# A cached-attention decode block on one core: the first softmax in pieces among K's last half tiles, three transfers fewer, and f32 matmuls without a reader

## The chip, the cores and the metric

The kernel runs on one core of a Trainium2 chip. The metric is the device time in microseconds of one execution. The core's engines work side by side, each through its own list of instructions in order: TensorE (PE; the loading of weights into it is shown as PEld), VectorE (DVE), ScalarE (ACT), GpSimd (POOL) and SyncE (SP), which here issues every transfer. The engines wait for each other and for transfers through semaphores. The profile also gives the granted TensorE clock: 1.0 is full speed, and the records of this kernel show 1.0 and 0.5.

## The reference, cut to what matters

One decode step for two batch elements, with 32 heads of 192, a window of the last 1024 keys, and a feed-forward layer after it; all inputs are bf16.

```python
mod = (silu(c) @ w_mod).reshape(2, 6, 1, 640)          # sa, ca, ga, sb, cb, gb
h = layernorm(x) * (1 + ca) + sa
q = (h @ wq).reshape(2, 1, 32, 192).transpose(0, 2, 1, 3)
k, v = k_cache[:, :, -1024:, :], v_cache[:, :, -1024:, :]
p = softmax(einsum('bhqd,bhkd->bhqk', q, k) * 192 ** -0.5)
o = einsum('bhqk,bhkd->bhqd', p, v)
x = x + ga * (o.transpose(0, 2, 1, 3).reshape(2, 1, 6144) @ wo)
h = layernorm(x) * (1 + cb) + sb
x = x + gb * ((gelu(h @ w_gate) * (h @ w_up)) @ w_down)
```

K and V of the window are 25.2 MB each, and with the weights 76.9 MB are read from HBM.

## The kernel before, in words

**Order.** A small planner (`_Sched`) collects operations; each engine's list is the order in which the code calls them. It works out from the buffers that an operation reads and writes what it must wait for. A PSUM bank counts as written by everyone who touches it. Nothing is reordered, so an operation that waits holds up everything behind it on its engine.

**Transfers.** All are issued by SP, in the order of the code, and go through one queue: w_mod, c and x, wq (7680 KB), then K of batch 0 in two loads of two tiles (6144 KB each), K of batch 1 in two, V of batch 0 in two, V of batch 1 in one load of two tiles and two loads of one tile (L336, L337), wo in four pieces of 16, 16, 12 and 4 of its 48 row tiles, w_gate, w_up, and w_down in three. A load waits on SP until the buffer that it fills has been read: the V loads wait for reduces of K, the last V loads for the first PV of batch 0, wo for the last PV of batch 0, the feed-forward weights for the first two PV of batch 1.

**Scores.** A cache tile has 128 partitions (32 heads by 4 groups of keys) with 64 keys of 192 each. Each tile is worked in two halves. For a half (b, t, hf), `d_mul` (L465, VectorE) multiplies K by the broadcast q in place, `p_reduce` (L476) adds up in TensorE with an identity as weights (12 matmuls of 512 columns), and `d_rows` (L483, VectorE) adds the rest from PSUM into `S_sb`. `scores` calls `d_rows` one half late, so VectorE multiplies the next half while TensorE reduces this one. Ahead of each reduce stands `filler()`: four bf16 matmuls of 384 columns whose result nobody reads (`warm`, L454).

**Softmax.** `softmax(b)` (L487) is a chain through three engines: pmax (DVE), a transpose on TensorE, max and gx (DVE), a broadcast matmul Bc, nb (DVE), exp (ACT), a matmul den, and its reciprocal rden (DVE). Both softmaxes run one after the other once all scores are done (L577, L578).

**PV and after.** `d_mask` (L511, VectorE) spreads a tile's probabilities over the heads into one of two buffers `Em`, `p_pv` (L523) multiplies by V with 32 matmuls. After batch 0's four tiles `normalize(0)` scales the result; after batch 1's, `normalize(1)`. `p_sel` puts both batches together, `oc` moves the result out of PSUM, three transposes `oT` (L597) on VectorE prepare 16 row tiles of wo each, and the wo matmuls (L628) follow by pieces. Then come the second layer norm (`layer_norm("ln2", 1, 3)`), the w_gate matmuls, gelu, the w_up matmuls, geglu (L660), its transpose, the w_down matmuls by pieces (L669), and the output. Between these stand further `warm` calls.

Of the kernel before, what the change touches and what calls it, by code (L numbers as in the profile page):

```python
# [5 lines left out]
ALU = mybir.AluOpType  # L6
ACTF = mybir.ActivationFunctionType
AX = mybir.AxisListType
# [95 lines left out]
def bass_adaLN_cond__sliding_block_cached__geglu_ffn__decode_kernel(  # L104
# [15 lines left out]
    P = 128  # L120
    B, _, D = A_x.shape
    _, H, Sk, Dh = A_k_cache.shape
# [9 lines left out]
    DN = D // NJ  # L132
# [3 lines left out]
    QP = P // H  # L136
# [10 lines left out]
    SCALE = float(Dh) ** -0.5  # L147
# [6 lines left out]
    NS = 4  # L154
    SL = J * Dh
    WQ_SPLIT = [5]
    assert sum(WQ_SPLIT) == KT
    WO_SPLIT = [16, 16, 12, 4]
    OT_SPLIT = [16, 16, 16]
    assert sum(WO_SPLIT) == NT and sum(OT_SPLIT) == NT  # L160
    WU_SPLIT = [5]
    assert sum(WU_SPLIT) == KT
    WD_SPLIT = [6, 4, 2]
    assert sum(WD_SPLIT) == FT
    ND = 4

    WO_WARM = [0, 8, 0, 9]
    WU_WARM = [5]
    WD_WARM = [5, 0, 0]

    es = ExitStack()
    with es:
        S = _Sched(nc, es)
# [45 lines left out]
        DS = sb("DS", [P, P], F32)  # L219
# [8 lines left out]
        modC = sb("modC", [P, 6, DN], F32)  # L228
# [10 lines left out]
        M1 = sb("M1", [P, 1], F32)  # L239
# [19 lines left out]
        def bank(k):  # L259
            return ("bank", k)  # L260
# [9 lines left out]
        sem_ring = [S.sem("d_ring%d" % i) for i in range(4)]  # L270
        sem_out = S.sem("d_out")

        def k_dma(dst, src):
# [49 lines left out]
        def ring_keys(slot):  # L323
# [10 lines left out]


        items = [("k", 0, 0, 2, 0, 0), ("k", 0, 2, 2, 2, 1), ("k", 1, 0, 2, NS, 2), ("k", 1, 2, 2, 0, 0), ("v", 0, 0, 2, 2, 1),  # L336
                 ("v", 0, 2, 2, NS, 2), ("v", 1, 0, 2, 0, 0), ("v", 1, 2, 1, 2, 1), ("v", 1, 3, 1, 3, 3)]  # L337
        place = {(kind, b, t0 + i): slot + i for kind, b, t0, nt, slot, _ in items for i in range(nt)}
        assert NTL == 4 and len(place) == 4 * NTL

# [109 lines left out]
        def warm(n, bk):  # L450
            def f(e):
                last = None
                for _ in range(n):
                    last = e.matmul(ps[:, bk, 0:2 * Dh], lhsT=ident_b[:, :], rhs=qbc[:, :, :].rearrange("p b d -> p (b d)"),  # L454
                                    start=True, stop=True)
                return last
            if n:
                S.op("pe", f, reads=["ident_b", "qbc"], writes=[bank(bk)], name="warm")
# [22 lines left out]
        def d_rows(b, t, hf):  # L481
            a = J * t + JH * hf
            S.op("dve", lambda e: e.tensor_reduce(out=S_sb[:, b, a:a + JH], in_=ps[:, hf, 0:JH * GC].rearrange("p (j c) -> p j c", j=JH),  # L483
                                                  axis=AX.X, op=ALU.add),
                 reads=[bank(hf)], writes=[("S", b, t, hf)], name="rows%d_%d_%d" % (b, t, hf))

        def softmax(b):  # L487
            sk = [("S", b, t, hf) for t in range(NTL) for hf in range(2)]
            S.op("dve", lambda e: e.tensor_reduce(out=M1[:, :], in_=S_sb[:, b, :], axis=AX.X, op=ALU.max),
                 reads=sk, writes=["M1"], name="pmax%d" % b)  # L490
            S.op("pe", lambda e: e.transpose(ps[0:1, BK_T, 0:P], M1[:, :], ident_f[:, :]),  # L491
                 reads=["M1", "ident_f"], writes=[bank(BK_T)], name="T%d" % b)
            S.op("dve", lambda e: e.tensor_reduce(out=gm[:, :], in_=ps[0:1, BK_T, 0:P].rearrange("k (h t) -> k h t", t=QP), axis=AX.X, op=ALU.max),
                 reads=[bank(BK_T)], writes=["gm"], name="max%d" % b)
            S.op("dve", lambda e: e.tensor_scalar(out=gx[:, :, :], in0=gm[:, :].unsqueeze(2).broadcast_to([1, H, QP]),
                                                  scalar1=-SCALE, scalar2=None, op0=ALU.mult),
                 reads=["gm"], writes=["gx"], name="gx%d" % b)
            S.op("pe", lambda e: e.matmul(ps[:, BK_T, P:P + 1], lhsT=gx[:, :, :].rearrange("k h t -> k (h t)"), rhs=one[:, :],  # L498
                                          start=True, stop=True),
                 reads=["gx", "one"], writes=[bank(BK_T)], name="Bc%d" % b)  # L500
            S.op("dve", lambda e: e.tensor_copy(out=nb[:, :], in_=ps[:, BK_T, P:P + 1]), reads=[bank(BK_T)], writes=["nb"], name="nb%d" % b)  # L501
            S.op("act", lambda e: e.activation(out=E_sb[:, b, :], in_=S_sb[:, b, :], func=ACTF.Exp, scale=SCALE, bias=nb[:, 0:1], accum_out=esum[:, b:b + 1]),  # L502
                 reads=sk + ["nb"], writes=[("E", b), ("esum", b)], name="exp%d" % b)
            S.op("pe", lambda e: e.matmul(ps[:, BK_T, P + 2:P + 3], lhsT=DS[:, :], rhs=esum[:, b:b + 1], start=True, stop=True),  # L504
                 reads=[("esum", b), "DS"], writes=[bank(BK_T)], name="den%d" % b)
            S.op("dve", lambda e: e.reciprocal(out=rden[:, b:b + 1], in_=ps[:, BK_T, P + 2:P + 3]),
                 reads=[bank(BK_T)], writes=[("rden", b)], name="rden%d" % b)


        def d_mask(b, t):  # L510
            S.op("dve", lambda e: e.tensor_tensor(out=Em[:, t % 2, :, :], in0=E_sb[:, b, J * t:J * (t + 1)].unsqueeze(2).broadcast_to([P, J, H]),  # L511
                                                  in1=M32b[:, :].unsqueeze(1).broadcast_to([P, J, H]), op=ALU.mult),
                 reads=[("E", b), "M32b"], writes=[("Em", t % 2)], name="mask%d_%d" % (b, t))

        def p_pv(b, t):
            vs = slot_of("v", b, t)
            n = J // 2

            def f(e):
                last = None  # L520
                for jp in range(n):
                    r = 2 * SQ * (jp % 2)
                    last = e.matmul(ps[r:r + 2 * H, BK_O, 0:ON],  # L523
                                    lhsT=Em[:, t % 2, 2 * jp:2 * jp + 2, :].rearrange("p j c -> p (j c)"),
                                    rhs=tile_v(vs)[:, 2 * jp:2 * jp + 2, :],
                                    start=(t == 0 and jp < 2), stop=(t == NTL - 1 and jp >= n - 2), tile_position=(0, r), skip_group_check=True)
                return last
            keep[("pv", b, t)] = S.op("pe", f, reads=[("Em", t % 2)] + ring_keys(vs), writes=[bank(BK_O)], name="PV%d_%d" % (b, t))
# [64 lines left out]
        for c in range(NQC):  # L593
            move(("act", "dve")[c % 2], oc[:, QC * c:QC * (c + 1)], ps[:, BK_H + c, 0:QC], [bank(BK_H + c)], [("oc", c)], "oc%d" % c)
# [121 lines left out]
```

## Time and profile before

| what | value |
|---|---|
| median of 3 runs | 187.17 us (187.05 to 187.21) |
| the profiled execution's own time | 187.01 us |
| its span, first to last instruction | 185.7 us |
| mean granted TensorE clock | 0.915 |
| PE busy | 117.2 us (63%) |
| DVE busy | 106.6 us (57%) |
| ACT busy | 13.9 us (7%) |
| moved by the DMA engines | 77.02 MB, mean 415 GB/s |

Busy times of different engines overlap, so they do not add up to the span. A line of the timeline gives start and length in us, the engine, the line of the code, the operation with what it writes and reads, how many instructions were merged (x12), and in brackets how long the engine was idle before and who released it. A row with x2 f32 under PE is one f32 matmul in the code: it appears as two records. Times in the text without another mark are counted from the start of the span.

### The profile page before, as it was taken

To read this page: it belongs to the slowest core of one execution; us is meant where nothing else is said; L and a number is where in the kernel's file an instruction comes from. 1 tells how busy PE (TensorE), PEld (TensorE's weight loads), DVE (VectorE), ACT (ScalarE), POOL (GpSimd) and SP (SyncE) were. 2 spreads that over 40 slices of the span, in tenths; PEclk is the share of its full clock that TensorE was granted. 3 is DMA by queue.
4 is the path that set the end of the run, shared out by engine and by line. 5 is a ranking of instruction groups with operands and counts; after the bars stand their busy time and mean duration, and the time that the engine had idled before them with its cause. 6 is when DMAs were issued, how large, how long until landed. Compare 5 with 4: busy or idle time off the path is not lost.

```text
span 185.7 us, 2254 instructions
## 1 busy us (share of the span) xinstructions
PE 117.2 (63%) x1014; PEld 60.8 (33%) x1014; DVE 106.6 (57%) x114; ACT 13.9 (7%) x24; POOL 4.9 (3%) x12
## 2 busy tenths in 40 slices
PE   0004500871079899988999885349928977299844
PEld 0001200440024334433344342226614654265422
DVE  6801600020598999999999993294556714803331
ACT  2001400013000000000000000200010004100400
POOL 8200000000000000000000000000000000000000
PEclk9999999998559999999999999558996999859999
DMA  7999998898999989899999989899999999999991
GB/s 248 414 437 477 463 463 389 371 491 371 487 413 434 468 381 459 381 487 402 455 424 434 459 381 466 381 487 413 395 434 424 424 435 424 413 408 435 422 392 50
DMA packets 2925, 77.02 MB, mean 415 GB/s; under 512 B 356, under 2 KB 356, under 8 KB 868
## 3 DMA queue, kind: packets, MB, share of 16 engines
q1 hardware_dynamic: 2916, 76.88, 96.7%
q8 instruction: 8, 0.13, 0.3%
q14 instruction: 1, 0.01, 0.0%
HBM read 76.88 MB, written 0.00 MB: 414 GB/s over the span
## 4 chain that ended last, share of the span: by engine, by line
DMA 43%; DVE 36%; PE 16%; SPq 1%; ACT 1%; issue 1%; POOL 1%; DVEq 0%; POOLq 0%
DMA ring<-in_A_k_cache_dram 24%; DVE ring L465 19%; DMA ring<-in_B_w_down_dram 18%; PE ps L523 10%; DVE r L465 7%; DVE Sg L483 5%; PE ps L476 4%; DVE Em L511 2%; SPq L274 1%; ACT E_sb L502 1%; PE ps L504 1%; PE ps L498 1%; DVE On L540 0%; ACT On L536 0%; PE ps L491 0%
## 5 line engine op out<-in xcount | busy, mean ns | idle before, releaser
L465 DVE TENSOR_TENSOR ring<-ring,qbc 128x6144 bf16<-128x6144 bf16 x12 | 40.1, 3351 | 8.4 <-DMA ring<-in_A_k_cache_dram 8.4
L476 PE MATMUL ps<-ring,ident_b 128*128 128x512 bf16 x144 | 34.7, 393 | 13.0 <-DVE ring L465 13.0
L454 PE MATMUL ps<-qbc,ident_b 128*128 128x384 bf16 x120 | 24.7, 339 | 0.7 <-ACT qbc L432 0.7
L523 PE MATMUL ps<-ring,Em 128*64 128x384 bf16 x192 | 19.6, 371 | 7.8 <-DVE Em L511 6.6
L476 PEld LDWEIGHTS ps<-ring,ident_b 128*128 128x128 bf16 x144 | 13.6, 100 | 32.7 <-DVE ring L465 17.2
L511 DVE TENSOR_TENSOR Em<-E_sb,M32b 128x2048 bf16<-128x2048 bf16 x8 | 18.1, 2288 | 5.5 <-PE ps L523 5.5
L523 PEld LDWEIGHTS ps<-ring,Em 128*64 128x64 bf16 x192 | 12.4, 125 | 14.6 <-DVE Em L511 7.3
L454 PEld LDWEIGHTS ps<-qbc,ident_b 128*128 128x128 bf16 x120 | 11.6, 101 | 10.9 <-issue 2.8
L401 PE MATMUL ps<-ring,scT 128*32 128x480 bf16 x40 | 4.4, 601 | 16.0 <-DVE scT L358 16.0
L465 DVE TENSOR_TENSOR r<-r,qbc 128x6144 bf16<-128x6144 bf16 x4 | 13.4, 3352 | 0.0
L483 DVE TENSOR_REDUCE Sg<-ps 128x32 f32<-128x512 f32 x16 | 11.0, 687 | 3.4 <-PE ps L476 3.4
L424 PE MATMUL ps<-r,hT 128*32 128x384 bf16 x80 | 5.8, 475 | 10.7 <-DMA r<-in_A_wq_dram 10.7
L476 PE MATMUL ps<-r,ident_b 128*128 128x512 bf16 x48 | 11.1, 380 | 1.8 <-DVE r L465 1.8
L434 DVE CAST aux<-ps 128x384 bf16<-128x384 f32 x4 | 2.0, 553 | 16.6 <-PE ps L424 15.7
L628 PE MATMUL ps<-r,aux 128*32 128x160 bf16 x192 | 5.1, 271 | 4.4 <-DMA r<-in_A_wo_dram 2.6
L424 PEld LDWEIGHTS ps<-r,hT 128*32 128x32 bf16 x80 | 3.2, 135 | 13.8 <-issue 11.6
L476 PEld LDWEIGHTS ps<-r,ident_b 128*128 128x128 bf16 x48 | 4.4, 98 | 8.1 <-DVE r L465 3.4
L401 PEld LDWEIGHTS ps<-ring,scT 128*32 128x32 bf16 x40 | 1.2, 132 | 17.5 <-DVE scT L358 16.0
L540 DVE TENSOR_SCALAR On<-ps,rden 32x192 bf16<-32x192 f32 x4 | 1.7, 418 | 8.9 <-ACT On L536 8.9
L502 ACT ACTIVATE E_sb<-Sg,nb 128x256 bf16<-128x256 f32 x2 | 1.0, 507 | 75.6 <-DVE nb L501 75.6
L628 PEld LDWEIGHTS ps<-r,aux 128*32 128x32 bf16 x192 | 4.3, 114 | 5.8 <-DMA r<-in_A_wo_dram 3.6
L523 PE MATMUL ps<-r,Em 128*64 128x384 bf16 x64 | 5.4, 327 | 0.0
(73 smaller groups left out, 65.6 us busy)
## 6 DMA issues: line engine op xcount, KB each, us to landing
ring<-in_A_k_cache_dram SPq DMA_DIRECT2D x3, 6144.0 KB, 40.3
ring<-in_A_v_cache_dram SPq DMA_DIRECT2D x2, 6144.0 KB, 23.3
r<-in_A_wq_dram SPq DMA_DIRECT2D x1, 7680.0 KB, 30.7
r<-in_A_k_cache_dram SPq DMA_DIRECT2D x1, 6144.0 KB, 38.4
r<-in_A_v_cache_dram SPq DMA_DIRECT2D x1, 6144.0 KB, 23.3
ring<-in_A_v_cache_dram SPq DMA_DIRECT2D x2, 3072.0 KB, 17.6
r<-in_A_wo_dram SPq DMA_DIRECT2D x2, 2560.0 KB, 23.7
ring<-in_w_mod_dram SPq DMA_DIRECT2D x1, 4800.0 KB, 14.2
```

Source lines behind the costliest of these rows:

```text
L274: return lambda e: e.dma_start(dst, src)
L401: last = e.matmul(ps[SQ * j:SQ * j + SQ, bk, 0:3 * DN].rearrange("p (i n) -> p i n", i=3), lhsT=scT[:, k, :], rhs=wm_v[:, k, 3 * part * D: ...
L424: last = e.matmul(ps[SQ * j:SQ * j + SQ, BK_H + c, 0:QC], lhsT=hT[:, k, :], rhs=wq_v[:, k, RN * j + QC * c:RN * j + QC * (c + 1)], start=( ...
L434: S.op("dve", lambda e: e.tensor_copy(out=dst, in_=src), reads=reads, writes=writes, name=name)
L454: last = e.matmul(ps[:, bk, 0:2 * Dh], lhsT=ident_b[:, :], rhs=qbc[:, :, :].rearrange("p b d -> p (b d)"), start=True, stop=True)
L465: S.op("dve", lambda e: e.tensor_tensor(out=tile_v(ks)[:, hf * JH:(hf + 1) * JH, :], in0=tile_v(ks)[:, hf * JH:(hf + 1) * JH, :], in1=qbc[ ...
L476: last = e.matmul(o_ap, lhsT=ident_b[:, :], rhs=tile_v(ks)[:, hf * JH:(hf + 1) * JH, ci * GC:(ci + 1) * GC], start=(ci == 0), stop=(ci == ...
L483: S.op("dve", lambda e: e.tensor_reduce(out=S_sb[:, b, a:a + JH], in_=ps[:, hf, 0:JH * GC].rearrange("p (j c) -> p j c", j=JH), axis=AX.X, ...
L502: S.op("act", lambda e: e.activation(out=E_sb[:, b, :], in_=S_sb[:, b, :], func=ACTF.Exp, scale=SCALE, bias=nb[:, 0:1], accum_out=esum[:, ...
L511: S.op("dve", lambda e: e.tensor_tensor(out=Em[:, t % 2, :, :], in0=E_sb[:, b, J * t:J * (t + 1)].unsqueeze(2).broadcast_to([P, J, H]), in ...
L523: last = e.matmul(ps[r:r + 2 * H, BK_O, 0:ON], lhsT=Em[:, t % 2, 2 * jp:2 * jp + 2, :].rearrange("p j c -> p (j c)"), rhs=tile_v(vs)[:, 2 ...
L628: last = e.matmul(ps[SQ * j:SQ * j + SQ, BK_M, 0:DN], lhsT=oT[:, t, :], rhs=wo_v[:, t, DN * j:DN * j + DN], start=(t == 0), stop=(t == NT ...
```

## The change

- `softmax(b)` returns four pieces. `scores(1, 0, 2, softmax(0))` calls one of batch 0's after each of the first four halves of batch 1, behind that half's `d_rows`. The pieces of batch 1's softmax are called between the first masks and PV of batch 0.
- The last two tiles of V of batch 1 are one transfer, and wo comes in two pieces of 32 and 16 row tiles instead of four: three transfers fewer, and two fewer stretches of wo matmuls.
- `warm` uses f32 operands and 480 columns instead of bf16 and 384. `filler()` is one such matmul instead of four; the other calls have 1 or 2 instead of 3 to 12. One call is new: `filler(7)` behind the second PV of batch 1.

```diff
-    WO_SPLIT = [16, 16, 12, 4]
+    WO_SPLIT = [32, 16]
...
-    ND = 4
-
-    WO_WARM = [0, 8, 0, 9]
-    WU_WARM = [5]
-    WD_WARM = [5, 0, 0]
+
+    WO_WARM = [2, 1]
+    WU_WARM = [1]
+    WD_WARM = [1, 0, 0]
...
-                 ("v", 0, 2, 2, NS, 2), ("v", 1, 0, 2, 0, 0), ("v", 1, 2, 1, 2, 1), ("v", 1, 3, 1, 3, 3)]
+                 ("v", 0, 2, 2, NS, 2), ("v", 1, 0, 2, 0, 0), ("v", 1, 2, 2, 2, 1)]
...
-                    last = e.matmul(ps[:, bk, 0:2 * Dh], lhsT=ident_b[:, :], rhs=qbc[:, :, :].rearrange("p b d -> p (b d)"),
+                    last = e.matmul(ps[:, bk, 0:3 * DN], lhsT=ident_f[:, :], rhs=modC[:, 0:3, :].rearrange("p i n -> p (i n)"),
                                     start=True, stop=True)
...
-            warm(n * ND, BK_W)
+            warm(n, BK_W)
...
         def softmax(b):
...
+            def piece_max():       # pmax, T
...
+            def piece_head():      # max, gx, Bc
...
+            def piece_exp():       # nb, exp
...
+            def piece_den():       # den, rden
...
+            return [piece_max, piece_head, piece_exp, piece_den]
...
-        def scores(b, ta, tb):
+        def scores(b, ta, tb, pieces=()):
+            pieces = list(pieces)
...
+                    if pieces:
+                        pieces.pop(0)()
...
-        scores(1, 0, 2)
+        scores(1, 0, 2, softmax(0))
...
-        softmax(0)
-        softmax(1)
-        weighted(0, 0, 2)
-        load_kv(9)
+        pieces = softmax(1)
+        pieces[0]()
+        d_mask(0, 0)
+        pieces[1]()
+        p_pv(0, 0)
+        d_mask(0, 1)
+        pieces[2]()
+        p_pv(0, 1)
+        pieces[3]()
+        load_kv(8)
         weighted(0, 2, 4)
...
             p_pv(1, t)
+            if t == 1:
+                filler(7)
             if t == NTL - 1:
                 p_sel(0)
         normalize(1)
-        warm(3, 1)
+        warm(1, 1)
         p_sel(1)
-        warm(6, 1)
+        warm(1, 1)
...
-        warm(12, 1)
+        warm(2, 1)
...
-        warm(8, 1)
+        warm(1, 1)
```

More of the change, by code (lines that the diff above doesn't have):

```diff
@@ L269, in bass_adaLN_cond__sliding_block_cached__geglu_ffn__decode_kernel @@
         sem_wd = [S.sem("d_wd%d" % i) for i in range(len(WD_SPLIT))]
-        sem_ring = [S.sem("d_ring%d" % i) for i in range(4)]
+        sem_ring = [S.sem("d_ring%d" % i) for i in range(3)]
         sem_out = S.sem("d_out")
@@ L457, in warm @@
             if n:
-                S.op("pe", f, reads=["ident_b", "qbc"], writes=[bank(bk)], name="warm")
+                S.op("pe", f, reads=["ident_f", ("modC", 0)], writes=[bank(bk)], name="warm")
         def filler(n=1):
-            warm(n * ND, BK_W)
+            warm(n, BK_W)
         def d_mul(b, t, hf):
@@ L488, in softmax @@
             sk = [("S", b, t, hf) for t in range(NTL) for hf in range(2)]
[L489 to L505, printed above, removed]
@@ L506, in softmax @@
-            S.op("dve", lambda e: e.reciprocal(out=rden[:, b:b + 1], in_=ps[:, BK_T, P + 2:P + 3]),
-                 reads=[bank(BK_T)], writes=[("rden", b)], name="rden%d" % b)
+            def piece_max():
+                S.op("dve", lambda e: e.tensor_reduce(out=M1[:, :], in_=S_sb[:, b, :], axis=AX.X, op=ALU.max),
+                     reads=sk, writes=["M1"], name="pmax%d" % b)
+                S.op("pe", lambda e: e.transpose(ps[0:1, BK_T, 0:P], M1[:, :], ident_f[:, :]),
+                     reads=["M1", "ident_f"], writes=[bank(BK_T)], name="T%d" % b)
@@ new lines, in piece_head @@
+            def piece_head():
+                S.op("dve", lambda e: e.tensor_reduce(out=gm[:, :], in_=ps[0:1, BK_T, 0:P].rearrange("k (h t) -> k h t", t=QP), axis=AX.X, op=ALU.max),
+                     reads=[bank(BK_T)], writes=["gm"], name="max%d" % b)
+                S.op("dve", lambda e: e.tensor_scalar(out=gx[:, :, :], in0=gm[:, :].unsqueeze(2).broadcast_to([1, H, QP]),
+                                                      scalar1=-SCALE, scalar2=None, op0=ALU.mult),
+                     reads=["gm"], writes=["gx"], name="gx%d" % b)
+                S.op("pe", lambda e: e.matmul(ps[:, BK_T, P:P + 1], lhsT=gx[:, :, :].rearrange("k h t -> k (h t)"), rhs=one[:, :],
+                                              start=True, stop=True),
+                     reads=["gx", "one"], writes=[bank(BK_T)], name="Bc%d" % b)
@@ new lines, in piece_exp @@
+            def piece_exp():
+                S.op("dve", lambda e: e.tensor_copy(out=nb[:, :], in_=ps[:, BK_T, P:P + 1]), reads=[bank(BK_T)], writes=["nb"], name="nb%d" % b)
+                S.op("act", lambda e: e.activation(out=E_sb[:, b, :], in_=S_sb[:, b, :], func=ACTF.Exp, scale=SCALE, bias=nb[:, 0:1], accum_out=esum[:, b:b + 1]),
+                     reads=sk + ["nb"], writes=[("E", b), ("esum", b)], name="exp%d" % b)
+            def piece_den():
+                S.op("pe", lambda e: e.matmul(ps[:, BK_T, P + 2:P + 3], lhsT=DS[:, :], rhs=esum[:, b:b + 1], start=True, stop=True),
+                     reads=[("esum", b), "DS"], writes=[bank(BK_T)], name="den%d" % b)
+                S.op("dve", lambda e: e.reciprocal(out=rden[:, b:b + 1], in_=ps[:, BK_T, P + 2:P + 3]),
+                     reads=[bank(BK_T)], writes=[("rden", b)], name="rden%d" % b)
```

## The prediction

> **What bounds the kernel now.** I read the page's slices and queues first, then the chain that ended last, then the timeline from 84 us to the end, then windows of 3.41 us, the step in which the granted clock changes in this trace.
>
> From the page (busy tenths in 40 slices, the granted clock, the DMA share, the bytes):
> ```profile
> PEclk9999999998559999999999999558996999859999
> DMA  7999998898999989899999989899999999999991
> HBM read 76.88 MB, written 0.00 MB: 414 GB/s over the span
> ```
> The DMA engines are full from 3 us to 182 us. The last pieces of the chain say the same:
> ```profile
> 148.89 33.92 DMA ring<-in_B_w_down_dram
> 182.81 0.04 issue
> 182.85 0.35 PE ps L669 x8
> ```
> The end is the landing of the last weight at 182.81 plus 2.9 us (8 matmuls, two VectorE steps, the store). So a shorter computation gains nothing. The question is whether the computation still keeps up, and the timeline shows where it is near:
> ```profile
> 95.21 2.76 PE L476 MATMUL ps<-r,ident_b 128*128 128x512 bf16 x12 [0.45 <-DVE r L465]
> 95.67 3.35 DVE L465 TENSOR_TENSOR ring<-ring,qbc 128x6144 bf16<-128x6144 bf16 x1
> 97.81 0.81 PE L454 MATMUL ps<-qbc,ident_b 128*128 128x384 bf16 x4
> ...
> 123.50 7.05 PE L523 MATMUL ps<-ring,Em 128*64 128x384 bf16 x64 [2.45 <-DVE Em L511]
> 130.41 5.39 PE L523 MATMUL ps<-r,Em 128*64 128x384 bf16 x64
> ...
> 150.84 2.79 PE L523 MATMUL ps<-ring,Em 128*64 128x384 bf16 x32 [1.14 <-DMA ring<-in_A_v_cache_dram]
> 159.08 1.29 PE L628 MATMUL ps<-r,aux 128*32 128x160 bf16 x64 [1.79 <-DVE aux L597]
> 162.78 2.33 PE L628 MATMUL ps<-r,aux 128*32 128x160 bf16 x64 [2.41 <-DMA r<-in_A_wo_dram]
> 169.00 0.46 PE L628 MATMUL ps<-r,aux 128*32 128x160 bf16 x16 [0.21 <-DMA r<-in_A_wo_dram]
> 174.09 1.00 PE L646 MATMUL ps<-ring,hT 128*32 128x384 bf16 x20 [0.61 <-DVE hT L358]
> 178.18 1.00 PE L646 MATMUL ps<-ring,hT 128*32 128x384 bf16 x20 [1.69 <-DMA ring<-in_B_w_up_dram]
> ```
> Each consumer in the second half waits for its transfer, but by little: 1.1 us at V's last tile, 2.4 at wo's second piece, 1.7 at w_up. Behind w_up there is almost nothing: w_up's matmuls at 178.18, geglu, its transpose and the down matmuls reach the last landing with some 0.4 us to spare. So the computation may reach w_up no later than about 178.4.
>
> The clock, in windows on its own steps (columns: window, length, PE busy, PEld, DVE, ACT, POOL, granted clock, DMA):
> ```profile
> 133.74:137.15 3.41, 2.07 (x26) 1.21 (x22) 0.41 (x1) 0.82 (x2) 0.00 (x0) 1.00 0.88 375
> 137.15:140.57 3.42, 0.58 (x8) 0.44 (x10) 3.36 (x3) 0.00 (x0) 0.00 (x0) 1.00 1.02 438
> 140.57:143.98 3.41, 3.41 (x26) 1.93 (x24) 1.56 (x1) 0.00 (x0) 0.00 (x0) 0.50 1.01 432
> 157.63:161.05 3.42, 1.29 (x64) 1.12 (x64) 3.42 (x3) 0.90 (x1) 0.00 (x0) 1.00 0.96 412
> 161.05:164.46 3.41, 1.68 (x52) 1.68 (x56) 0.56 (x1) 0.00 (x0) 0.00 (x0) 0.50 1.02 427
> ```
> A window with 0.58 or 1.29 us of matmuls is followed by half clock, one with 2.07 is not; half clock ends after a window that was full (140.57), not after one with 1.68.
>
> The profiled execution took 187.01 us, 1.3 around its span of 185.7; the median of the runs is 187.17, 0.16 above it. I add changes to the median.
>
> **The change, part by part.**
>
> Three transfers fewer. Transfers of 6144 KB land 14.54 us apart, one of 640 KB takes 1.57: proportional to size, but for 0.06 us each. Ends: 0 and 0.1. Three give -0.19 at the end, if the end stays the DMA's. The merged V transfer lands at 150.6, where the second half did; its first tile, which was there at 143, now comes with it.
>
> The first softmax in the scores. The pieces stand behind the halves (1,0,0), (1,0,1), (1,1,0), (1,1,1). On VectorE, which paces this stage (3.27 + 0.60 per half against TensorE's 2.76 + 0.65): pmax 0.33, max 0.31, gx 0.23, nb 0.17, together 1.05. The transpose and the broadcast stand on TensorE behind reduces that VectorE awaits anyway in its next rows step: no wait. The last piece is different: its den matmul stands on TensorE behind the reduce of (1,1,1), and its reciprocal stands on VectorE in the same piece, ahead of the multiply of (1,2,0). That reduce starts when the multiply of (1,1,1) ends, so VectorE does 0.60 of rows and then waits until 0.05 + 2.76 + 0.38 (den, as the stat matmul at L369) + 0.17: 2.8 us lost, with every later half behind it. TensorE then stands idle some 2.5 us; at half clock the next reduce is late by up to 1.0: I take 0.5. Sum: the last reduce ends at 113.44 + 1.05 + 2.8 + 0.5 = 117.8. SP issues the V load that waits for it 4.4 later, at 117.9; the queue ahead drains at 119.4 (fastest engine) to 121.4 (slowest), so this is covered, by 1.5 us on the fastest. The merged V load waits for the second PV of batch 0, 129.3 in the sum below against a queue that drains at 134; the weights' loads have over 10 us.
>
> f32 matmuls. TensorE shows an f32 matmul as two records; none in this trace has more than 2 columns of this kind. Lower end: two passes at bf16's rate (0.16 per 384 columns), 2 x 0.20 = 0.40. Upper end: two records as long as the longest of 480 columns, 601 ns at L401: 1.2. I take the middle, 0.80. The Trainium skill has a price (Perfetto Trace Analysis, Engine Utilization): output at half rate for FP32_LOW_HIGH, which for two records is also 0.80 and would leave the sum as it is; no run here shows it. In the scores 2.76 + 0.80 stays under 3.87 and costs nothing; the cover is gone at 1.1.
>
> From the last reduce on, in order (before's time in brackets):
> - rows and pmax 1.06, the first mask 2.20 before max and gx 0.54, broadcast 0.6: the first PV at 122.2 (123.50). The second softmax's rest is beside it.
> - The two PV as before 7.05: 129.3. Then den, and rden on VectorE ahead of the third mask: 0.5 + 2.29, PV at 132.1 (130.41). TensorE idles 2.3 us of that, so I take one window at half clock: 5.39 + 1.7, end 139.2 (135.80).
> - normalize, two masks, two PV: 135.80 to 147.08 was 11.28; end 150.5.
> - Seven f32 matmuls without a reader, 5.6, ahead of PV(1,2) in TensorE's order: 156.1. V has landed at 150.6, so PV(1,2) waits for nothing but them. This is the largest term. Ends 2.8 and 8.4.
> - Two PV 5.4: 161.5 (153.63).
> - To wo's first matmul 5.45 as before, plus 1.36 since the first piece of 32 needs two transposes: 168.3 (159.08). wo has landed.
> - 128 matmuls: 2.4 at full clock, 4.7 at half. The gap before them is over 3 us as before's, so mostly half: 4.0. End 172.3.
> - Two f32 matmuls 1.6, the 64 of the second piece 1.3: 175.2 (169.46).
> - ln2 to hT, 4.63: 179.8 (174.09). w_gate 0.84, filler 0.80, w_up 1.00: 182.5 (179.18).
> - geglu and transpose 1.56, down0 0.42, filler 0.8, the last two 0.6: 185.9 (183.20).
>
> Difference 2.7; the tail after it is unchanged. Span 188.4, time 187.17 + 2.7 = 189.9. I round down to **189.8**, as the clock terms were taken rather high.
>
> **Rivals.**
>
> The chain stays hidden. If none of the new gaps halves the clock, the sum loses 0.5 + 1.7 + 1.6, and wo's second piece ends near 171.4: w_up's matmuls can start at 177.7, before the landing at 178.0. Then the end is the DMA's and the time 187.17 - 0.19 = 186.98: this is the point from which it decides. For it: the gaps are 2.3 to 2.8 us and the window's phase may cut them. Against it: 1.29 us of matmuls did not hold the clock at 157.6. The Trainium skill (TensorE: Matmul & The Clock Gate, Part 1) lets the clock fall after an idle window of about 3.4 us; by that the short gaps cost nothing and it ends here; the trace's windows with 0.58 and 1.29 us of matmuls speak against so strict a reading.
>
> Cheap f32 matmuls (0.40): the chain loses 4.4 and is hidden too, 186.98; nothing in the profile excludes it.
>
> Hidden, and the slowest DMA engine better off: 8 instruction transfers (0.13 MB, 0.3% of 16 engines' span: 1.1 us each, on one engine) share the queues, and the last transfer's 16 landings spread over 1.8 us. Fewer instructions on TensorE could spare the slowest engine some 0.3: 186.7, faster.
>
> f32 matmuls at 1.2 or more: TensorE paces the scores, the 7 cost 8.4, the chain is 4 to 8 later: 194 to 198.
>
> **Numbers.** What can be told from no change is about 0.2%, 0.37 us. Chain late as summed, +1 to +5: 0.60. Late by less, +0.4 to +1: 0.06. Dear f32, above +5: 0.08. Hidden at 186.98 (full clock or cheap f32): 0.17. Hidden and below 186.8: 0.09. So slower 0.74, same 0.17, faster 0.09. The range drops most of the last on both sides: 186.9 to 192.6; the likeliest case alone has 188.2 to 192.2.
>
> **What would show it.** VectorE idle about 2.8 us before the reciprocal near 99 us, released by TensorE; the seven f32 matmuls at 150 to 156, and PV(1,2) not waiting for a DMA; w_gate's matmuls after 178; the chain that ended last running through wo and ln2 in place of the w_down transfer. Wrong if w_up's matmuls still wait for their landing, if the seven take under 4 us, or if the granted clock stays at 1.0 from 127 on.

## The result, and the profile after

The changed kernel takes 191.44 us (median, 191.14 to 192.35) beside 187.11 us for the kernel before on the same chip: a ratio of 1.0237, with a 95% interval of 1.021 to 1.0264. It is 4.3 us slower. The prediction was 189.8 us, slower by 2.6. The direction, the place and most of the terms held; the time came out 1.6 above it.

The profiled execution after took 191.46 us, its span is 190.2. From its page, the granted clock and the DMA share in 40 slices:

```profile
PEclk9999999998559999999999699759995899988999
DMA  7899998989989999899998998998989999999930
```

The last slice but one of DMA is now 3 and the last 0: the same 76.88 MB have landed some 6 us before the end. The kernel is no longer waiting for its last weight. The chain that ended last (start, length in us, engine and line; xN are instructions) runs through the computation instead:

```profile
123.15 7.89 PE ps L533 x64
131.04 0.33 PE ps L512 x2
131.39 0.17 DVE rden L514
131.56 2.20 DVE Em L521
133.80 5.41 PE ps L533 x64
...
143.38 8.05 PE ps L533 x64
151.43 5.83 PE ps L453 x14
157.26 5.34 PE ps L533 x64
...
169.38 3.98 PE ps L649 x96
173.36 1.81 PE ps L453 x4
...
181.03 1.00 PE ps L667 x20
182.02 1.00 PE ps L453 x2
183.02 0.96 PE ps L667 x20
...
187.17 0.56 PE ps L690 x24
```

L533 are the PV matmuls, L453 the matmuls without a reader, L649 wo, L667 w_gate and w_up, L690 the w_down matmuls. The seven new f32 matmuls stand on this chain with 5.83 us (x14, two records each). The V tiles of the PV behind them have landed at 152.01, 0.6 us after the first of the seven begins. No step behind 123 waits for a transfer. Ahead of this part, the timeline of the scores shows the other new wait, and what it delays (in brackets: idle before, and who released it):

```profile
97.17 2.76 PE L475 MATMUL ps<-r,ident_b 128*128 128x512 bf16 x12 [0.36 <-DVE r L464]
99.77 0.28 PE L512 MATMUL ps<-esum,DS 128*128 128x1 f32 x2
100.08 0.17 DVE L514 RECIPROCAL rden<-ps 128x1 f32<-128x1 f32 x1 [2.37 <-PE ps L512]
103.56 4.45 PE L475 MATMUL ps<-ring,ident_b 128*128 128x512 bf16 x12 [2.60 <-DVE ring L464]
118.77 12.89 SPq L273 DMA_DIRECT2D ring<-in_A_v_cache_dram  x2
```

VectorE stands 2.37 us idle in front of the first reciprocal, since den stands on TensorE behind a whole reduce. The next reduce starts late and runs at half clock, 4.45 in place of 2.76. The V load that waits for K's last reduce is issued at 118.77, not at 113.52 (the row merges it with the next load). The windows show the clock (columns: window, length, busy us of PE, PEld, DVE, ACT and POOL, granted clock, DMA share, GB/s):

```profile
101.03:104.45 3.42, 0.89 (x5) 0.42 (x6) 3.42 (x3) 0.00 (x0) 0.00 (x0) 1.00 0.90 388
104.45:107.86 3.41, 3.41 (x10) 1.40 (x9) 2.92 (x1) 0.00 (x0) 0.00 (x0) 0.50 1.04 447
118.10:121.51 3.41, 0.86 (x4) 0.18 (x2) 2.75 (x3) 0.00 (x0) 0.00 (x0) 1.00 0.87 288
121.51:124.93 3.42, 2.36 (x14) 1.57 (x16) 3.23 (x5) 0.12 (x1) 0.00 (x0) 0.50 0.96 417
```

In the third row the DMA engines move 288 GB/s: the queue ran empty ahead of the late V load. Two shorter windows show where (a packet counts in the window in which it starts):

```profile
119.00:120.00 1.00, 0.07 (x1) 0.07 (x1) 0.97 (x3) 0.00 (x0) 0.00 (x0) 1.00 0.12 49
120.00:121.00 1.00, 0.20 (x1) 0.01 (x1) 1.00 (x1) 0.00 (x0) 0.00 (x0) 1.00 2.24 688
```

By the landing records, the 16 engines finished the transfer ahead of it at 119.55 (fastest) to 121.75. By the packet records, the first packets of the V load start at 120.10, 1.33 us after its issue, and the first ones on most engines take 2.3 to 2.9 us where a packet on the full queue takes 1.82. The load's 6144 KB take 14.54 us on a full queue; here the first engine's landing, at 135.61, is 16.84 us after the issue, 2.3 more, and 1.5 later than it would be behind the landing at 119.55. The last weight landed at 184.09, against 182.81 before.

### The profile page after: what moved, and what is told of

It reads as the page before. It is cut to its first block, busy times and chain, and to the rows that moved or that the text cites. A ratio compares the mean times of both kernels' runs of the same rounds, so it can differ in the third digit from the quotient of the medians.

```text
span 190.2 us, 2135 instructions
## 1 busy us (share of the span) xinstructions
PE 125.4 (66%) x960; PEld 61.8 (32%) x960; DVE 106.3 (56%) x114; ACT 13.9 (7%) x24; POOL 4.9 (3%) x12
## 3 DMA queue, kind: packets, MB, share of 16 engines
q1 hardware_dynamic: 2484, 76.88, 94.5%
HBM read 76.88 MB, written 0.00 MB: 404 GB/s over the span
## 4 chain that ended last, share of the span: by engine, by line
DVE 39%; PE 32%; DMA 24%; issue 1%; ACT 1%; POOL 1%; SPq 0%; DVEq 0%; POOLq 0%
DMA ring<-in_A_k_cache_dram 24%; DVE ring L464 17%; PE ps L533 14%; PE ps L475 8%; DVE r L464 7%; PE ps L453 5%; DVE Sg L482 4%; DVE Em L521 4%; PE ps L649 3%; DVE aux L618 1%; PE ps L667 1%; DVE On L550 1%; ACT On L546 1%; PE ps L690 1%; DVE aux L433 1%
## 5 line engine op out<-in xcount | busy, mean ns | idle before, releaser
L475 PE MATMUL ps<-ring,ident_b 128*128 128x512 bf16 x144 | 36.8, 410 | 15.4 <-DVE ring L464 15.4
L453 PE MATMUL ps<-modC,ident_f 128*128 128x480 f32 x66 | 31.7, 581 | 0.0
L475 PEld LDWEIGHTS ps<-ring,ident_b 128*128 128x128 bf16 x144 | 14.1, 104 | 40.5 <-DVE ring L464 22.8
L533 PE MATMUL ps<-ring,Em 128*64 128x384 bf16 x192 | 21.4, 396 | 4.2 <-DVE Em L521 4.2
L533 PEld LDWEIGHTS ps<-ring,Em 128*64 128x64 bf16 x192 | 12.7, 134 | 12.8 <-DVE Em L521 4.6
L453 PEld LDWEIGHTS ps<-modC,ident_f 128*128 128x128 f32 x66 | 11.7, 192 | 6.8 <-issue 4.6
L423 PE MATMUL ps<-r,hT 128*32 128x384 bf16 x80 | 4.9, 419 | 11.0 <-DMA r<-in_A_wq_dram 11.0
L649 PE MATMUL ps<-r,aux 128*32 128x160 bf16 x192 | 5.3, 289 | 3.3 <-DVE aux L618 3.3
L533 PE MATMUL ps<-r,Em 128*64 128x384 bf16 x64 | 5.4, 327 | 2.5 <-DVE Em L521 2.5
L649 PEld LDWEIGHTS ps<-r,aux 128*32 128x32 bf16 x192 | 4.9, 124 | 4.7 <-issue 4.7
```

The costliest lines, as they stand in the source:

```text
L423: last = e.matmul(ps[SQ * j:SQ * j + SQ, BK_H + c, 0:QC], lhsT=hT[:, k, :], rhs=wq_v[:, k, RN * j + QC * c:RN * j + QC * (c + 1)], start=( ...
L453: last = e.matmul(ps[:, bk, 0:3 * DN], lhsT=ident_f[:, :], rhs=modC[:, 0:3, :].rearrange("p i n -> p (i n)"), start=True, stop=True)
L475: last = e.matmul(o_ap, lhsT=ident_b[:, :], rhs=tile_v(ks)[:, hf * JH:(hf + 1) * JH, ci * GC:(ci + 1) * GC], start=(ci == 0), stop=(ci == ...
L533: last = e.matmul(ps[r:r + 2 * H, BK_O, 0:ON], lhsT=Em[:, t % 2, 2 * jp:2 * jp + 2, :].rearrange("p j c -> p (j c)"), rhs=tile_v(vs)[:, 2 ...
L649: last = e.matmul(ps[SQ * j:SQ * j + SQ, BK_M, 0:DN], lhsT=oT[:, t, :], rhs=wo_v[:, t, DN * j:DN * j + DN], start=(t == 0), stop=(t == NT ...
```

## The experiments

Ratios are against the kernel before the change, run on the same chip. Each experiment computes the whole reference.

### e1: the changed kernel without the seven f32 matmuls

```diff
             p_pv(1, t)
-            if t == 1:
-                filler(7)
```

> The changed kernel without the seven f32 matmuls behind the second PV of batch 1. Theory (TensorE's chain is late, and the seven are its largest term, 5.83 us): PV of the third tile starts at 151.5 to 152 instead of 157.2 and the chain reaches the end some 5 us earlier; the last landing, at 184.1 in the changed kernel because the V load was issued late, then sets the end: 188.0 to 188.5 us, about +1.1 over the kernel before. Rival (the half clock makes the loss, and the seven keep the clock up): without them the clock falls behind the PV and the time stays above 190. Rival (the queue's empty stretch makes the whole loss): the time stays near 191.

Measured 188.41 us, ratio 1.0058 (1.0037 to 1.0079), as expected. The chain that ended last:

```profile
153.64 30.54 DMA ring<-in_B_w_down_dram
184.17 0.04 issue
```

The end is the DMA's again, with a landing at 184.17 that is 1.36 later than before. So the seven are worth about 3.0 of the 4.3 us (191.44 less 188.41; the two medians come from different chips), though they take 5.83: without them the computation ends under the last landing, and the rest of them was slack. The other 1.2 us belong to the rest of the change, and here they are a later landing, not a longer computation. That is what the empty queue predicts.

### e4: fourteen in place of seven

```diff
-                filler(7)
+                filler(14)
```

> The changed kernel with fourteen f32 matmuls in place of the seven. Theory: all of the added 5.6 us lies on the path to the end: 196.5 to 197.5 us, 5 to 6 above the changed kernel. Rival (the seven stand beside a wait or pay for themselves in clock): under 194.

Measured 196.3 us, ratio 1.0494 (1.0464 to 1.0524): 4.9 above the changed kernel, a little under the 5 to 6. From its timeline:

```profile
103.98 2.76 PE L475 MATMUL ps<-ring,ident_b 128*128 128x512 bf16 x12 [2.60 <-DVE ring L464]
122.52 7.04 PE L533 MATMUL ps<-ring,Em 128*64 128x384 bf16 x64
132.32 7.07 PE L533 MATMUL ps<-r,Em 128*64 128x384 bf16 x64 [2.45 <-DVE Em L521]
143.57 6.76 PE L533 MATMUL ps<-ring,Em 128*64 128x384 bf16 x64 [4.18 <-DVE Em L521]
150.26 11.54 PE L453 MATMUL ps<-modC,ident_f 128*128 128x480 f32 x28
```

Fourteen take 11.54, 0.82 each: twice the seven, all on the path, near the 0.80 that was forecast. The added matmuls take 5.6 and the time grew by 4.9; the missing 0.8 lies ahead of them. They begin at 150.26 where the seven began at 151.36, in a code that is the same up to there. The reduce behind the den wait ran at full clock this time (2.76 against 4.45), and the three stretches of PV took 7.04, 7.07 and 6.76 against 7.96, 5.39 and 8.05. The same gaps lose the clock in one execution at one place and in the next at another: the window of 3.41 us that holds the den wait has 1.45 us of matmuls here and 0.89 in the changed kernel's profile, by where the window's edges fall.

### e2: the reciprocal one half later

den stays where it is; the first softmax's reciprocal stands behind the next half, when den has long been done.

```diff
             def piece_den():
...
+            def piece_rden():
                 S.op("dve", lambda e: e.reciprocal(out=rden[:, b:b + 1], in_=ps[:, BK_T, P + 2:P + 3]),
...
-            return [piece_max, piece_head, piece_exp, piece_den]
+            return [piece_max, piece_head, piece_exp, piece_den, piece_rden]
...
-        scores(1, 0, 2, softmax(0))
+        pieces = softmax(0)
+        scores(1, 0, 2, pieces[:4])
...
-        scores(1, 2, 4)
+        scores(1, 2, 4, pieces[4:])
...
         pieces[3]()
+        pieces[4]()
```

> The changed kernel with the first softmax's reciprocal one half later on VectorE, its den matmul where it was. Theory: VectorE's wait of 2.37 us near 100 us goes, TensorE's idle stretch there and its half clock with it, so the last reduce ends at 115.0 to 115.8 instead of 118.7, the next V load is issued while the queue still holds work, and the transfers end at 182.6. The seven f32 matmuls stay, so the chain is 3 to 3.5 us earlier than in the changed kernel: 187.3 to 188.3 us, +0.2 to +1.2. Rival (only the seven matter): over 190.5.

Measured 188.62 us, ratio 1.0057 (1.0027 to 1.0086), in a wide spread, 186.88 to 189.44. The median is above the 187.3 to 188.3 that was expected, the mechanism as expected:

```profile
101.12 0.15 DVE L516 RECIPROCAL rden<-ps 128x1 f32<-128x1 f32 x1
115.15 0.54 SPq L273 DMA_DIRECT2D ring<-in_A_v_cache_dram  x1
148.39 5.90 PE L453 MATMUL ps<-modC,ident_f 128*128 128x480 f32 x14
```

No idle time in front of the reciprocal, the V load is issued 3.6 us earlier, the last weight lands at 182.79 as before the change. With the seven still there the computation ends last, so the 2.8 us that this one line saves come off the end. The 1.4 us that are left go in e3, which takes out the seven and moves the second reciprocal too; no run parts these two.

### e3: both mended

e2 without the seven, and the second softmax's reciprocal moved behind the last mask of batch 0 as well (the edit is shown against e2).

```diff
         pieces[3]()
-        pieces[4]()
         load_kv(8)
         weighted(0, 2, 4)
+        pieces[4]()
...
-            if t == 1:
-                filler(7)
```

> The changed kernel without the seven and with both softmaxes' reciprocals later (the first one half later, the second behind the last mask of batch 0). Theory: the chain is hidden again and the end is the DMA's, with three transfers fewer at 0.06 us each: 186.7 to 187.0 us, 0.1 to 0.4 below the kernel before. Rival (f32 matmuls without a reader or fewer wo pieces hold the end in themselves): 188 or more.

Measured 187.15 us, ratio 1.0002 (0.9987 to 1.0017), against 186.7 to 187.0 expected: level, not faster. The profiled execution (187.72 us) is one of the longer ones, and its timeline has what went wrong there:

```profile
150.88 7.95 PE L535 MATMUL ps<-ring,Em 128*64 128x384 bf16 x64 [5.42 <-DMA ring<-in_A_v_cache_dram]
```

Its windows show the clock there (columns as above):

```profile
145.89:149.30 3.41, 0.00 (x0) 0.00 (x0) 1.98 (x1) 0.00 (x0) 0.00 (x0) 1.00 1.00 432
149.30:152.71 3.41, 1.83 (x12) 1.26 (x14) 0.00 (x0) 0.00 (x0) 0.00 (x0) 0.50 0.92 396
```

The merged transfer brings V's last two tiles together. TensorE, now early, waits 5.42 us for them, a whole window is empty, and the two PV run at half clock, 7.95 against 5.39. That is a wait which matmuls without a reader could fill (f4 tries it). In the changed kernel it hardly exists: behind the late scores TensorE reaches this place at 151.4, when V is just landing (its last engine at 152.0), and the seven come on top but for 0.6 us.

### e5: the three transfers alone

```diff
-    WO_SPLIT = [16, 16, 12, 4]
+    WO_SPLIT = [32, 16]
...
-    WO_WARM = [0, 8, 0, 9]
+    WO_WARM = [8, 9]
...
-                 ("v", 0, 2, 2, NS, 2), ("v", 1, 0, 2, 0, 0), ("v", 1, 2, 1, 2, 1), ("v", 1, 3, 1, 3, 3)]
+                 ("v", 0, 2, 2, NS, 2), ("v", 1, 0, 2, 0, 0), ("v", 1, 2, 2, 2, 1)]
```

> The kernel before with the three transfers fewer alone (V's last two tiles in one, wo in 32 and 16; 8 and 9 bf16 matmuls without a reader behind the wo pieces). Theory (0.06 us for each transfer on every DMA engine, and the chain stays hidden though PV of the third tile now waits for 150.6): -0.1 to -0.25 us. Rival (a transfer's cost is hidden in the queue): 0.0. Rival (the later PV makes the chain late): +0.3 or more.

Measured 187.74 us, ratio 1.0047 (1.0022 to 1.0073), with single times from 187.02 to 189.58. It was expected to gain 0.1 to 0.25, and loses; the rival, that the later V makes the chain late, has it. In the profiled execution (188.84 us), the rows are

```profile
152.34 7.07 PE L523 MATMUL ps<-ring,Em 128*64 128x384 bf16 x64 [2.81 <-DMA ring<-in_A_v_cache_dram]
166.20 3.67 PE L628 MATMUL ps<-r,aux 128*32 128x160 bf16 x128 [3.13 <-DVE aux L597]
```

PV waits 2.81 us for V and then takes 7.07, and wo's 128 matmuls mostly run at half clock too (3.67). The chain passes through V's landing at 152.20 and stays on the computation to the end. Part of the late landing is again the queue: the kernel before issues the first of the two single loads at 128.04, behind the first PV of batch 0. The merged load waits for the second PV as well; in this execution it was issued at 132.43, and the fastest engine ran dry at about 134. The fastest engine's two landings lie 15.4 us apart where 14.54 are usual.

### e6: the f32 matmuls alone

Every warm-up matmul in f32 with 480 columns, in the counts of the change, without the seven.

```diff
-    WU_WARM = [5]
-    WD_WARM = [5, 0, 0]
+    WU_WARM = [1]
+    WD_WARM = [1, 0, 0]
...
-                    last = e.matmul(ps[:, bk, 0:2 * Dh], lhsT=ident_b[:, :], rhs=qbc[:, :, :].rearrange("p b d -> p (b d)"),
+                    last = e.matmul(ps[:, bk, 0:3 * DN], lhsT=ident_f[:, :], rhs=modC[:, 0:3, :].rearrange("p i n -> p (i n)"),
...
-        warm(8, 1)
+        warm(1, 1)
```

> The kernel before with the matmuls without a reader in f32 of 480 columns alone, in the changed kernel's numbers (1 for each 4 in the scores; 1, 1, 2, 1, 2, 1, 1, 1 after it) and without the new seven. Theory (each takes 0.80 us, about as much as the five bf16 that it stands for, and the scores stay paced by VectorE): within 0.2 us of the kernel before. Rival (f32 matmuls slow the scores or the tail by themselves): +0.5 or more. Rival (fewer instructions mean fewer instruction transfers on the DMA engines): -0.2 to -0.4.

Measured 187.70 us, ratio 1.0034 (1.0022 to 1.0046), where no difference was expected; the size is that of the rival, that f32 slows the tail by itself. Its windows near the end:

```profile
175.25:178.66 3.41, 1.64 (x22) 0.58 (x18) 0.00 (x0) 0.49 (x1) 0.00 (x0) 1.00 0.99 406
178.66:182.08 3.42, 3.42 (x38) 1.25 (x34) 1.42 (x2) 0.00 (x0) 0.00 (x0) 0.50 0.72 291
```

The timeline at the second of them:

```profile
178.27 1.45 PE L646 MATMUL ps<-ring,hT 128*32 128x384 bf16 x20 [1.77 <-DMA ring<-in_B_w_up_dram]
179.65 1.97 PE L454 MATMUL ps<-modC,ident_f 128*128 128x480 f32 x2
```

One f32 matmul behind w_gate is shorter than the eight bf16 ones that it replaces. The window ahead of w_up holds 1.64 us of matmuls and the clock falls on the last stretch, where there was hardly any slack: one f32 matmul takes 1.97.

### f2: e6 with two f32 matmuls behind w_gate

```diff
-        warm(1, 1)
+        warm(2, 1)
```

> The kernel of e6_f32 (f32 without a reader alone) with two instead of one behind the w_gate matmuls. Theory (in e6_f32 the clock fell at 178.7 since one f32 of 1.07 us left its window with 1.65 us of matmuls where eight bf16 had left 1.79): the clock stays up to the end and the time falls from 187.7 to that of the kernel before, within 0.2 us. Rival (f32 matmuls delay the tail by themselves): 187.6 or more.

Measured 187.20 us, ratio 1.0005 (0.9996 to 1.0013), level as expected. Its windows at the same place:

```profile
174.00:177.40 3.40, 2.80 (x24) 1.12 (x24) 0.35 (x1) 0.49 (x1) 0.00 (x0) 1.00 0.98 411
177.40:180.80 3.40, 2.00 (x22) 0.74 (x22) 1.41 (x2) 0.00 (x0) 0.00 (x0) 1.00 0.95 389
```

Neither stretch is short of matmuls now and the clock stays at 1.00. (They do not lie on the clock's own steps; on these, 175.17 to 178.58 has 2.45 us of matmuls.) So e6's loss is the clock at this one place, not f32 as such.

### e7: the softmax in pieces alone

The kernel before with the four pieces and the new order of the second softmax, nothing else.

```diff
-        scores(1, 0, 2)
+        scores(1, 0, 2, softmax(0))
...
-        softmax(0)
-        softmax(1)
-        weighted(0, 0, 2)
+        pieces = softmax(1)
+        pieces[0]()
+        d_mask(0, 0)
+        pieces[1]()
+        p_pv(0, 0)
+        d_mask(0, 1)
+        pieces[2]()
+        p_pv(0, 1)
+        pieces[3]()
```

> The kernel before with the softmax in pieces alone, as in the changed kernel. Theory: VectorE's wait for den costs 2.4 to 2.8 us and one reduce at half clock, so the V load after the last reduce is issued 4 to 5 us later, the queue runs empty for 1 to 1.5 us and the transfers end 0.8 to 1.3 us later: +0.7 to +1.4 us, with the end set by the last transfer. Rival (the wait stays covered by the queue, as the prediction had it): 0.0. Rival (the pieces gain what they are moved for): below -0.2.

Measured 188.55 us, ratio 1.0079 (1.0061 to 1.0098), 1.5 us slower, just above the 0.7 to 1.4 that were expected. The reciprocal and the V load in its timeline:

```profile
100.35 0.17 DVE L514 RECIPROCAL rden<-ps 128x1 f32<-128x1 f32 x1 [2.37 <-PE ps L512]
118.27 0.54 SPq L274 DMA_DIRECT2D ring<-in_A_v_cache_dram  x1
```

The end of the chain that ended last:

```profile
152.10 32.16 DMA ring<-in_B_w_down_dram
184.26 0.04 issue
```

The same 2.37 us, with no fallen clock here (the next reduce took 2.76), and the last landing at 184.26, 1.45 later than before. The V load's first packets start 1.32 us after its issue, and it landed on the fastest engine at 135.06, 2.25 us more after its issue than the 14.54 that it takes on a full queue. The pieces cost nothing on the computation that shows; they cost because one transfer is issued 4.75 us later.

### f1: the pieces alone, with both reciprocals later

The edit is shown against e7.

```diff
-            return [piece_max, piece_head, piece_exp, piece_den]
+            return [piece_max, piece_head, piece_exp, piece_den, piece_rden]
...
-        scores(1, 0, 2, softmax(0))
+        pieces = softmax(0)
+        scores(1, 0, 2, pieces[:4])
...
+        scores(1, 2, 4, pieces[4:])
...
+        pieces[4]()
```

> The kernel before with the softmax pieces alone, and both reciprocals later (the first one half later, the second behind the last mask of batch 0); transfers and bf16 matmuls as before. Theory (of the pieces alone, +1.5 us in e7_pieces, all comes from VectorE's wait for den): the queue never runs empty, the chain is earlier than before by some 3 us, which gains nothing, and the time is that of the kernel before: -0.1 to +0.1 us. Rival (the pieces cost something else in the scores): +0.5 or more. Rival (an earlier chain gains): below -0.2.

Measured 187.17 us, ratio 1.0007 (0.9998 to 1.0015), as expected. The V load goes out at 115.73, 3.8 us ahead of the landing in front of it, and the last weight lands at 182.92. Against e7 the only difference is where two small reciprocals stand: 1.4 us.

### e8 and f3: what a transfer costs

e8 cuts wo into twelve pieces, eight transfers more; f3 into two, two fewer, with V's last tiles apart as before. The bf16 matmuls without a reader stay behind the same row tiles.

```diff
-    WO_SPLIT = [16, 16, 12, 4]
+    WO_SPLIT = [4] * 12
...
-    WO_WARM = [0, 8, 0, 9]
+    WO_WARM = [0, 0, 0, 0, 0, 0, 0, 8, 0, 0, 0, 9]
```

> The kernel before with wo in 12 transfers of 4 row tiles instead of 4. Theory (0.06 us for each of 8 more): +0.4 to +0.6 us. Rival (a transfer costs nothing when the queue is full): 0.0 to 0.1.

```diff
-    WO_SPLIT = [16, 16, 12, 4]
+    WO_SPLIT = [32, 16]
...
-    WO_WARM = [0, 8, 0, 9]
+    WO_WARM = [8, 9]
```

> The kernel before with wo in two transfers (32 and 16) alone, V's last two tiles still in two. Theory (in e5_transfers the loss came from V: both tiles' PV wait for the joint landing): two transfers at 0.08 us fewer and the chain hidden, -0.1 to -0.2 us. Rival (wo's large first piece makes the chain late): +0.3 or more, and unsteady as in e5_transfers.

e8 measured 187.73 us, ratio 1.004 (1.0028 to 1.0052): 0.72 us for eight, 0.09 each, more than the 0.4 to 0.6 that were expected, and its last landing is 0.63 later, 0.08 each. f3 measured 186.97 us, ratio 0.9993 (0.9984 to 1.0002): -0.12 for two, the expected sign and size, though the interval does not leave out zero, and in its profiled execution the last weight lands at 182.85, no earlier than before. A transfer more costs under 0.1 us; that a transfer less gains as much is not shown.

### f4: a version that keeps the parts

The changed kernel with both reciprocals later as in e3, six f32 matmuls in place of the seven, where the joint landing is awaited, and two behind w_gate. The reciprocals' edit is not repeated here.

```diff
-                filler(7)
+                filler(6)
...
-        warm(1, 1)
+        warm(2, 1)
```

> The changed kernel mended: both reciprocals later, six instead of seven f32 behind the second PV of batch 1, where TensorE otherwise stands idle from 145.5 to 150.9, and two instead of one behind the w_gate matmuls. Theory: PV of the third tile starts at 150.9 to 152 at full clock (e3_both had it at half), the chain is hidden, and the three transfers fewer give -0.2 to -0.35 us: 186.7 to 186.9. Rival (V's joint landing is too late in any case): above the kernel before.

Measured 186.90 us, ratio 0.9993 (0.9982 to 1.0003), within the 186.7 to 186.9 that were expected. From its timeline:

```profile
144.77 5.10 PE L453 MATMUL ps<-modC,ident_f 128*128 128x480 f32 x12
150.80 5.39 PE L535 MATMUL ps<-ring,Em 128*64 128x384 bf16 x64 [0.93 <-DMA ring<-in_A_v_cache_dram]
178.13 1.00 PE L671 MATMUL ps<-ring,hT 128*32 128x384 bf16 x20 [0.48 <-DMA ring<-in_B_w_up_dram]
```

The six end 0.93 us before V lands: they fill the wait and delay nothing, and PV keeps the clock (5.39). The w_up matmuls wait for their landing again. With the reciprocals moved, six for seven and one matmul more behind w_gate, the change goes from 191.4 to 186.9. Whether f4 beats the kernel before, by 0.1 or 0.2 us, is not clear of the noise.

## Why the prediction came out as it did

**The main line held.** The end went from the last landing to the computation, through the seven, wo and the second layer norm, as the likeliest case said. The largest term, seven f32 matmuls, was put at 5.6 between ends of 2.8 and 8.4; they took 5.83, and e1 and e4 show that they decide. The middle value of 0.80 for one was nearly right: 14 records in 5.83 are 0.42 each, 0.83 for a matmul. The Trainium skill (Perfetto Trace Analysis, Engine Utilization) has half the output rate for FP32_LOW_HIGH. Read for each of the two records, the trace agrees: 0.42 for a record of 480 columns, about twice the 0.20 that was worked out from bf16's rows. For a whole matmul it is four times, and the trace does not name the mode.

**The sum, step by step** (ends in us of the span):

| step | predicted | measured |
|---|---|---|
| last reduce of K ends | 117.8 | 118.71 |
| first PV starts | 122.2 | 123.15 |
| two PV of batch 0 end | 129.3 | 131.04 |
| four PV of batch 0 end | 139.2 | 139.21 |
| two PV of batch 1 end | 150.5 | 151.43 |
| the seven end | 156.1 | 157.26 |
| wo starts | 168.3 | 169.38 |
| wo ends | 175.2 | 176.42 |
| hT is there | 179.8 | 181.03 |
| w_up's matmuls end | 182.5 | 183.98 |
| last w_down matmul ends | 185.9 | 187.73 |

**The start of the scores was taken as given, and it isn't.** 0.9 of the 1.8 us are there at the first row of the table, and 1.0 was there before the change did anything: K's first load lands at another time in each execution, and the first reduce runs at half clock for a varying part. The first rows of the scores in the timeline of before:

```profile
48.61 6.63 DVE L465 TENSOR_TENSOR ring<-ring,qbc 128x6144 bf16<-128x6144 bf16 x2 [8.41 <-DMA ring<-in_A_k_cache_dram]
52.03 4.33 PE L476 MATMUL ps<-ring,ident_b 128*128 128x512 bf16 x12 [8.71 <-DVE ring L465]
```

The same rows of after:

```profile
49.20 6.63 DVE L464 TENSOR_TENSOR ring<-ring,qbc 128x6144 bf16<-128x6144 bf16 x2 [10.07 <-DMA ring<-in_A_k_cache_dram]
52.62 4.74 PE L475 MATMUL ps<-ring,ident_b 128*128 128x512 bf16 x12 [11.02 <-DVE ring L464]
```

The first reduce ended at 56.36 and at 57.36. Over the fourteen profiled executions of this study it ended between 56.4 and 57.8, and before's was the earliest of all: by luck the sum was added to the best start. Where the DMA sets the end this is hidden; where the computation does, it is in the time. With that 1.0 the prediction's terms for the pieces, 1.05 + 2.8 + 0.5, give 118.8 for the last reduce, against 118.71.

**The clock was taken at the wrong places.** The prediction put one half window, 1.7, on the third and fourth PV; those ran at full clock (5.41). The window that holds the gap before them, 131.75 to 135.17, has 1.37 us of matmuls and was not followed by half clock. Instead the first two took 7.89 where 7.05 was kept, and the stretch from there to the end of the first two PV of batch 1 (139.21 to 151.43) took 12.22 where 11.28 was kept. At 139.2 the late start (0.9), the slower first two PV (0.8) and the half window that did not come (1.7) cancel, which is luck; then 0.9 is added. Over the whole the three errors of the clock cancel, so the 1.8 us are the start and the f32 matmuls below. That gaps of some 2.4 us cost clock somewhere was right; where, changes from run to run (e4).

**A lone f32 matmul on the chain takes 1.0, not 0.8.** One stands between w_gate and w_up and one ahead of the last w_down pieces, with 1.00 each in the chain; with 0.2 at wo (1.81 for two) and 0.2 in the seven this is 0.8 us of the sum.

**"This is covered, by 1.5 us on the fastest" failed.** The prediction took a load as covered when it is issued before the queue is empty. The landings say otherwise. Issued 0.8 us ahead of the landing in front of it, the V load lost 1.5 us; issued 1.2 ahead in e7 and 1.5 ahead in e5, a load lost 1.1 and 0.9; issued 3.8 ahead in f1, it lost nothing. The estimate from these is that it has to be issued some 2.3 us ahead. The last landing moved by 1.28, with e1 and e7 at about the same 184.2, and came back when the reciprocal moved (e2, f1). The computation was longer still in the changed kernel, so the total doesn't show it. But the rival "the chain stays hidden", 186.98, did not exist as priced: with the chain hidden the time is 188.4 (e1), slower too. The chance of 0.17 for no change stood on this step.

**The merged V load was costed at its transfer alone.** The prediction gave its landing, 150.6, and its first tile's delay, and no price for either, with the seven as cover. The profiled executions of e5 and e3 show the price without the cover: a wait of 2.8 and 5.4 us and a fallen clock behind it. In the changed kernel this V landed at 152.0 and not at 150.6, behind the late load ahead of it.

**f32 for bf16 was costed at nothing outside the chain's rows.** e6 has +0.7 for it, a fallen clock at w_up. It is not visible in the changed kernel, which is late there for other reasons.

**The three transfers** were put at 0.06 each; e8 has 0.08 to 0.09. In the changed kernel this gains nothing, since the end is not the DMA's.

The parts alone cost 0.7 (transfers), 0.7 (f32), 1.5 (pieces), and the seven 3.0 on top of the rest: 5.9 in all for a total of 4.3. They do not add up; the likely reason is that each is measured against the same slack between computation and last landing. The second reciprocal was not tested alone: in the changed kernel TensorE stands idle for 2.45 us around it (up to 133.80), and in f4, where both are moved, that gap is gone.

## What to carry to other kernels

On an in-order engine, put the reader of a result one step behind the step in which it is produced: two reciprocals, 0.17 us each, cost 1.4 us where they stood (e7 against f1). When the transfers set the end, ask of each load how long before the queue runs dry it is issued, and count the restart; ask of each merged load whether its first part was needed early and whether it now waits for a later reader. Matmuls that only keep the clock have to fit the wait that they fill, measured with the rest of the change in place: six fit (f4), seven at the end of a longer chain cost about 3 us (e1).

## What the runs showed of the hardware

- **Restart of an empty queue.** When a load was issued to a queue that was running dry, its first packets started 1.3 us after the issue (1.33 in the changed kernel, 1.32 in e1, e4, e5 and e7), and many of these took 2.3 to 3.0 us in place of 1.82. From the issue to the first engine's landing, it took 2.25 to 2.34 us more than on a full queue in four of these runs and 2.80 in e4, while on a full queue a transfer more costs 0.08 to 0.09 us. The Trainium skill (DMA: Bandwidth & Descriptors, Anatomy of one DMA — SWDGE (gpsimd) path) puts the fixed cost of one transfer at about 2.0 us; the transfers here are issued by SP, and what a load took here beyond its time on a full queue is near that figure.
- **The clock falls without an idle window.** Windows of 3.41 us with 0.89, 0.86 and 1.64 us of matmuls were followed by half clock; one with 1.79, in the kernel before at 174.7, was not. Over the windows at full clock in the fourteen traces, all with up to 1.33 us of matmuls were followed by half clock, some with 1.37 to 1.65 were and some were not (1.37 at 131.75 in the changed kernel and 1.45 at 102.02 in e4 were not), and none with 1.76 or more was. The Trainium skill (TensorE: Matmul & The Clock Gate, Part 1: The HAM clock gate) has the clock fall after an idle window of about 3.4 us; in these rows it falls after windows with matmuls in over a third of them (1.33 of 3.41). Between 1.37 and 1.65 the busy time alone does not settle it, and what does is open.
- **A chain at its limit spreads the times.** Where the DMA set the end of the profiled execution, single times lie within 0.5 to 1.3 us (f1: 186.89 to 187.41; e7: 187.75 to 189.01). Where the computation is close to it, they lie within 1.2 to 2.6 (e3: 186.76 to 187.95; e5: 187.02 to 189.58; e2: 186.88 to 189.44): the start of the scores and the place of the clock's windows differ in each execution. That these two make up the whole spread was not tested.
